# FNet mixing and a low-rank mixer: symmetric DFT tables from fewer sines, odd part of batch 0 folded first, weights' loads placed behind batch 0, last chunk stored by single tiles

## The chip, the cores and the metric

One core of one Trainium2 chip runs the program alone. The metric is device time in microseconds (us) per execution; the time before is the median of three runs. One more execution was taken with the hardware profiler, and all views below are of that one.

## The reference

x is 8 x 3136 x 256 in float32. A two-dimensional Fourier transform over rows and channels gives its real part, then a mixer adds a product of rank 32 along the rows, and a two-layer product along the channels:

```python
X = np.fft.fft(x, axis=1)
X = np.fft.fft(X, axis=2)
x = X.real
xt = x.transpose(0, 2, 1)
h = xt @ U @ V                         # U 3136 x 32, V 32 x 3136
u = x + h.transpose(0, 2, 1)
ch = np.maximum(u @ w_ch1, 0.0) @ w_ch2   # 256 x 1024 and 1024 x 256
out = u + ch
```

## The kernel before

The real part of the transform is (cosine over rows)(cosine over channels) minus (sine)(sine). The kernel makes the tables on the chip, folds the input by symmetry so that each product is short, and transforms with matmuls.

**Input.** For a batch b, `load_x(b)` brings x into `xf` (rows forward, two halves a, gathered by POOL's indirect DMAs, L52) and into `xr` (rows backward, plain loads on SP's queue, L69). `load_0` fills one more partition of both by two small loads on SP (L75, L78). There is one buffer of each, so the next batch's load waits until the fold has read them. U's loads (`uf`, `ur`) run ahead of x's on the same queues.

**Tables.** `tabs[0]` (sine; named tabs in the profile) and `tabs[1]` (cosine; tabc) have 99 partitions, eight row groups i, two frequency parities, and 393 frequencies plus 32 columns. `phase` (VectorE, L139 and L141) makes an angle per element into `ph`; `sine` (ScalarE, L146) is one activation from it, `cosine` two: an absolute value (L152) and a sine (L153). Each of the eight groups is computed in full width, 2 x 393. `halve` (L201) scales the last group. `transform_u` multiplies the tables with the folded U (`fold_u`, L164 to L169) on TensorE (L194) and copies the result into the table's 32 last columns (L196, L197), so that the transform of x also yields the low-rank part.

**Fold.** `fold(b)` on VectorE: `along_d` takes differences (L217) and sums (L218) of mirrored channels from xf into `eof` and from xr into `eor`, and ScalarE copies the two lone channels (L215); `mirror` combines `eof` and reversed `eor` into `eos` (L222, L224); `half` (L228) adds or subtracts the two row halves into `G[b % 2][parity]`. G has the odd (difference) part in columns 0:128, the even (sum) part in 128:256, and the two lone channels in 256:258 with zeros behind them.

**Transforms.** `seq(b, par, typ, pn)` multiplies G with the tables (L279), typ 1 from G's even part (4 matmuls into A), typ 0 from its odd part and the lone channels (4 + 4 matmuls into B). pn = 0 is copied by ScalarE (`ev`, L283), and VectorE combines both pn into A or B (L292 to L297). The order is par 0 typ 1, par 0 typ 0, par 1 typ 1, par 1 typ 0. `chan` does the channel transform (L304 with A, L306 with B, copies L308 into S and T), with its sine and cosine tables `msn` and `mc` made from `pd` in the start and two sign memsets of msn on VectorE (L258, L259). `lowrank` makes TA and one row of VA (L320).

**Chunks.** The output is made in 49 chunks of 512 rows: `front(c)` adds the low-rank part (L342, L350), `first_product` is L362 with the ReLU L364 on ScalarE, `second_product` is L376 into a PSUM pair `p2` of two 128-row tiles; VectorE adds the residual (L382, L384, L385), and one store per chunk goes out on SP (L388).

**Order.** The source writes batch 0 out ahead of everything; then a table `due` spreads each later batch's fold, load and transforms over the chunks of the batch before it. The weights are loaded by POOL's queue behind the first transforms in the source: W1's upper half (L414), W1's lower half gathered in reverse and cast (`w1t`, L52 and L420), W2 (L421), V (L429). The framework sets all semaphores and lays out each engine's queue when the program is built; an instruction need not stand in a queue where the source has it.

Of the kernel before, what the change touches and what calls it, by code (L numbers as in the profile page):

```python
# [16 lines left out]
P = 128  # L17
PQ = 98
# [9 lines left out]
def kernel(  # L28
# [108 lines left out]
    def phase(y, a_ap, col_ap, bits):  # L137

        nc.vector.tensor_scalar(y.bitcast(FP32), a_ap, col_ap, float(2 ** (23 - bits)),  # L139
                                op0=AL.mult, op1=AL.add)  # L140
        nc.vector.tensor_single_scalar(y, y, 2 ** bits - 1, op=AL.bitwise_and)  # L141

    def sine(out_, y, bits, sgn):
        unit = TWO_PI / 2 ** bits
        pp = out_.shape[0]
        nc.scalar.activation(out_, y, AF.Sin, scale=-sgn * unit,  # L146
                             bias=(c_pi if sgn > 0 else c_npi)[:pp])

    def cosine(out_, y, bits):
        pp, free = y.shape  # L150
        ab = gen.tile([pp, free], FP32, tag="ab", name="ab")
        nc.scalar.activation(ab[:], y, AF.Abs, bias=c_half[bits][:pp])  # L152
        nc.scalar.activation(out_, ab[:] if len(out_.shape) == 2 else  # L153
                             ab.rearrange("p (a q) -> p a q", a=2), AF.Sin,
                             scale=TWO_PI / 2 ** bits, bias=c_nhp[:pp])

    kflat = krow.rearrange("p a q -> p (a q)")
    ph = gen.tile([KP, NI, 2 * NQ], I32, name="ph", bufs=1)
    uo = cpool.tile([KP, 2, NI, R], FP32, name="uo")
    ue = cpool.tile([KP, 2, NI, R], FP32, name="ue")  # L160
    GU = [cpool.tile([KP, 2, NI, R], BF16, name=f"gu{par}", tag=f"gu{par}") for par in range(2)]
# [20 lines left out]

    def transform_u(typ):

        for pk in range(2):
            pu = psum.tile([P, NI, R], FP32, tag="dft", name="pu", bufs=3)
            for io in range(NI):
                pn = (io + 1) % 2
                m = kp(io)
                j0 = NQ - 1 - (4 * 97 + (io + 1) // 2)  # L190
                ks = ktiles(pk)
                for n, i in enumerate(ks):
                    w = tabs[typ][:kp(i), i, pn, j0:j0 + 4 * (m - 1) + 1:4]
                    nc.tensor.matmul(pu[:m, io, :], w, GU[pn][:kp(i), typ, i, :],  # L194
                                     start=(n == 0), stop=(n == len(ks) - 1))
# [5 lines left out]
        nc.vector.tensor_single_scalar(tabs[t][:, NI - 1, :, :NQ], tabs[t][:, NI - 1, :, :NQ],  # L201
                                       hv[:KP], op=AL.mult)

    for i in range(NI):
        phase(ph[:, i], kflat[:KP], ncol[:KP, i:i + 1], 15)
        sine(tabs[0][:, i, :, :NQ], ph[:, i].rearrange("p (a q) -> p a q", a=2), 15, 1)
    fold_u()
    halve(0)
    transform_u(0)
    for i in range(NI):  # L210
        cosine(tabs[1][:, i, :, :NQ], ph[:, i], 15)
    def fold(b):

        def along_d(a, src, dst):
            nc.scalar.copy(dst[:, a, :, 128:257:128], src[:, a, :, 0:129:128])  # L215
            lo, hi = src[:, a, :, 1:128], src[:, a, :, 255:128:-1]
            nc.vector.tensor_tensor(dst[:, a, :, 1:128], lo, hi, op=AL.subtract)  # L217
            nc.vector.tensor_tensor(dst[:, a, :, 129:256], lo, hi, op=AL.add)  # L218

        def mirror(a):  # L220
            rv = EOR_[:, a, ::-1]
            nc.vector.tensor_tensor(EOS[:, a, :, 0:128], EOF_[:, a, :, 0:128], rv[:, :, 0:128],  # L222
                                    op=AL.subtract)
            nc.vector.tensor_tensor(EOS[:, a, :, 128:258], EOF_[:, a, :, 128:258],  # L224
                                    rv[:, :, 128:258], op=AL.add)

        def half(par):
            nc.vector.tensor_tensor(G[b % 2][par][:, :, 0:258], EOS[:, 0], EOS[:, 1],  # L228
                                    op=AL.add if par == 0 else AL.subtract)

        for a in range(2):
            yield lambda a=a: along_d(a, xf, EOF_)
            yield lambda a=a: along_d(a, xr, EOR_)
            yield lambda a=a: mirror(a)
        yield lambda: half(0)
        yield lambda: half(1)

    for step in fold(0):
        step()
    halve(1)  # L240
    transform_u(1)


    lrow = cpool.tile([P, 2, P], FP32, name="lrow")
    pcol = cpool.tile([P, 1], FP32, name="pcol")
    nc.gpsimd.iota(lrow[:], pattern=[[0, 2], [1, P]], base=0, channel_multiplier=0,
                   allow_small_or_imprecise_dtypes=True)
    nc.gpsimd.iota(pcol[:], pattern=[[0, 1]], base=0, channel_multiplier=1,
                   allow_small_or_imprecise_dtypes=True)
# [8 lines left out]
    nc.vector.memset(msr[:, :, 0:1], 1.0)  # L258
    nc.vector.memset(msr[:, :, 1:2], -1.0)  # L259
    MDT = [MSN, MC]  # L260

    def seq(b, par, typ, pn):

# [100 lines left out]
        nc.scalar.activation(k["h"][:, j, :], p1[:], AF.Relu)  # L364

    def second_product(c, t):
        k = CK[c]
        h, ut = k["h"], k["ut"]
        if t == 0:
            k["o"] = cp.tile([P, CH // P, D], FP32, tag="o", name="o", bufs=2)  # L370
        if t % 2 == 0:
            k["p2"] = psum.tile([P, 2, D], FP32, tag="p2", name="p2", bufs=2)
        o, p2 = k["o"], k["p2"]
        rs = slice(t * P, (t + 1) * P)
        for j in range(JT):
# [111 lines left out]
```

## Time and profile before

| what | us |
|---|---|
| median of 3 runs (lowest, highest) | 508.53 (507.36, 508.66) |
| the profiled execution | 507.78 |
| its span, first to last instruction | 506.0 |
| PE busy | 475.2 (94%) |
| VectorE (DVE) busy | 309.5 (61%) |
| ScalarE (ACT) busy | 288.7 (57%) |
| POOL busy | 38.7 (8%) |
| first product (L362) starts | 54.58 |
| last output add (L385) ends | 501.68 |

The page divides the span into 40 slices of 12.65 us; each digit is the busy share in tenths:

```profile
PE   0559999999999999999999999999999999999995
DVE  8874999999999776963474345344343344343432
```

In a list by order of time a line gives start, length, engine, line of the kernel, operation and tiles, the count of merged instructions, and in brackets how long the engine idled before it and what released it. In a list of waits the three numbers are the sum, the count and the longest. PEld is TensorE's weight load; a name with q is a queue's own instruction.

### The profile page before, as it was taken

How to read it: one execution, taken by the hardware profiler on the slowest of the kernel's cores; microseconds unless marked ns; L12 is line 12 of the kernel's file. 1: busy time of each engine (PE TensorE's matmuls, PEld its weight loads, DVE VectorE, ACT ScalarE, POOL GpSimd, SP SyncE). 2: the span in 40 equal slices, each digit the busy share in tenths (PEclk: the TensorE clock that was granted, in tenths of full speed). 3: DMA queues.
4: the chain of work that ended last, by engine and by line, in shares of the span. 5: the costliest groups of instructions: out<-in, count | busy, mean ns of one | idle time of the engine just before them, and what ended most of it. 6: DMA issues, size and time to landing. Idle time of an engine off the chain costs nothing.

```text
span 506.0 us, 8152 instructions
## 1 busy us (share of the span) xinstructions
PE 475.2 (94%) x3152; PEld 305.7 (60%) x3152; DVE 309.5 (61%) x681; ACT 288.7 (57%) x565; POOL 38.7 (8%) x45
## 2 busy tenths in 40 slices
PE   0559999999999999999999999999999999999995
PEld 0544466666666666666666666666666666666664
DVE  8874999999999776963474345344343344343432
ACT  6672754766466644755456544755466545665561
POOL 8250111002120100000000000000000000000000
PEclk9999999999999999999999999999999999999998
DMA  7856786789959982334223342333224322333442
GB/s 207 185 135 155 131 239 183 212 233 244 225 168 228 297 212 93 92 99 121 64 62 84 105 83 62 105 85 105 62 63 99 104 71 63 104 87 107 120 115 93
DMA packets 83422, 67.13 MB, mean 133 GB/s; under 512 B 53418, under 2 KB 79856, under 8 KB 80232
## 3 DMA queue, kind: packets, MB, share of 16 engines
q1 hardware_dynamic: 79816, 51.86, 39.0%
q0 software_dynamic: 3568, 14.76, 11.2%
q8 instruction: 24, 0.39, 0.3%
q14 instruction: 14, 0.11, 0.1%
HBM read 29.26 MB, written 25.69 MB: 109 GB/s over the span
## 4 chain that ended last, share of the span: by engine, by line
PE 93%; ACT 3%; DMA 1%; DVE 1%; POOL 0%; issue 0%; DVEq 0%; POOLq 0%; ACTq 0%
PE p L376 34%; PE p L362 34%; PE pt L279 14%; PE ph L342 4%; PE pu L194 2%; PE pst L306 2%; PE pst L304 2%; DMA uf<-in_moe_U_dram,xidx 1%; ACT ab L152 1%; ACT tabc L153 1%; PE ptt L316 1%; DVE tabs L201 0%; ACT S L308 0%; ACT T L308 0%; POOL uf L52 0%
## 5 line engine op out<-in xcount | busy, mean ns | idle before, releaser
L364 ACT ACTIVATE h<-p 128x512 bf16<-128x512 f32 x392 | 218.3, 597 | 141.7 <-PE p L362 141.6
L362 PE MATMUL p<-u,w 128*128 128x512 bf16 x784 | 209.7, 379 | 0.6 <-DVE u L350 0.5
L376 PE MATMUL p<-w,h 128*128 128x256 bf16 x1568 | 203.5, 273 | 0.0
L376 PEld LDWEIGHTS <-h 128*128 128x128 bf16 x1568 | 153.3, 98 | 59.0
L362 PEld LDWEIGHTS <-w 128*128 128x128 bf16 x784 | 75.7, 98 | 63.4 <-issue 3.3
L382 DVE TENSOR_TENSOR o<-p,ut 128x4 f32<-128x4 f32 x98 | 15.9, 162 | 138.5 <-PE p L376 137.0
L279 PE MATMUL pt<-tabc,g 98*128 98x425 bf16 (+1 forms) x256 | 58.0, 352 | 0.4 <-ACT tabc L196 0.4
L279 PEld LDWEIGHTS <-g 98*128 98x128 bf16 (+1 forms) x384 | 38.1, 99 | 31.3 <-issue 3.7
L384 DVE TENSOR_TENSOR o<-p,ut 128x254 f32<-128x254 f32 x98 | 40.2, 411 | 0.0
L385 DVE TENSOR_TENSOR o<-p,ut 128x254 f32<-128x254 f32 x98 | 40.2, 410 | 0.0
L283 ACT COPY ev<-pt 128x425 f32<-128x425 f32 x32 | 16.5, 516 | 36.7 <-PE pt L279 27.4
L350 DVE TENSOR_TENSOR u<-ph,S 128x512 bf16<-128x512 f32 (+15 forms) x64 | 34.9, 555 | 0.9 <-PE ph L342 0.9
L350 DVE TENSOR_TENSOR u<-ph,T 128x512 bf16<-128x512 f32 (+15 forms) x64 | 34.8, 554 | 0.0
L52 POOL DMA_INDIRECT xf<-in_x_dram,xidx x16 | 23.3, 1455 | 123.5 <-ACT h L364 69.9
L342 PE MATMUL ph<-va,ta 128*128 128x512 bf16 (+18 forms) x128 | 29.3, 329 | 0.6 <-ACT ta L319 0.6
L279 PE MATMUL pt<-tabs,g 98*128 98x425 bf16 (+1 forms) x128 | 29.1, 350 | 0.0
L292 DVE TENSOR_TENSOR B<-pt,ev 128x393 bf16<-128x393 f32 (+1 forms) x16 | 9.3, 584 | 24.5 <-PE pt L279 24.2
L306 PE MATMUL pst<-B,msn 128*128 128x392 bf16 (+1 forms) x64 | 20.9, 330 | 0.4 <-DVE B L292 0.4
L304 PE MATMUL pst<-A,mc 128*128 128x392 bf16 (+1 forms) x64 | 21.0, 331 | 0.1
L308 ACT CAST S<-pst 128x392 bf16<-128x392 f32 (+1 forms) x32 | 15.8, 493 | 8.8 <-PE pst L306 8.7
L217 DVE TENSOR_TENSOR eof<-xf 99x1016 bf16<-99x1016 f32 x16 | 19.3, 1206 | 2.3 <-DMA xf<-in_x_dram 2.0
L292 DVE TENSOR_TENSOR A<-pt,ev 128x393 bf16<-128x393 f32 (+1 forms) x16 | 9.4, 589 | 17.8 <-PE pt L279 17.8
(79 smaller groups left out, 278.0 us busy)
## 6 DMA issues: line engine op xcount, KB each, us to landing
out_dram<-o SPq DMA_DIRECT2D x49, 512.0 KB
xr<-in_x_dram SPq DMA_DIRECT2D x16, 784.0 KB
ut<-u SPq DMA_TRANSPOSE x49
w<-in_moe_w_ch_dram POOLq DMA_DIRECT2D x1, 512.0 KB, 13.0
va<-in_moe_V_dram POOLq DMA_DIRECT2D x2, 196.0 KB, 3.2
xf<-in_x_dram,xidx POOLq DMA_INDIRECT x16, 8.8
w<-in_moe_w_ch_dram POOLq DMA_DIRECT2D x1, 256.0 KB, 12.4
ur<-in_moe_U_dram SPq DMA_DIRECT2D x1, 196.0 KB
```

Of the source, the lines that this page charges most:

```text
L52: nc.gpsimd.indirect_dma_start(out_, None, bass.AP(t.tensor, t.offset, [[w, rows], [1, w]]), bass.IndirectOffsetOnAxis(idx, 0), element_of ...
L217: nc.vector.tensor_tensor(dst[:, a, :, 1:128], lo, hi, op=AL.subtract)
L279: nc.tensor.matmul(pt[:], g[:kp(i), i, col:col + P], tabs[t][:kp(i), i, par, :], start=(n == 0), stop=(n == len(mm) - 1))
L304: nc.tensor.matmul(pt[:, :hi - lo], MC[:, h * P:(h + 1) * P], d["A"][:, lo:hi], start=True, stop=False)
L306: nc.tensor.matmul(pt[:, :hi - lo], MSN[:, h * P:(h + 1) * P], d["B"][:, lo:hi], start=False, stop=True)
L342: nc.tensor.matmul(ph[:, col:col + hi - lo], TA[b % 2][:, s * P:(s + 1) * P], VA[b % 2][:, lo:hi], start=True, stop=True)
L350: nc.vector.tensor_tensor(u[:, s, col:col + hi - lo], ph[:, col:col + hi - lo], src, op=AL.add)
L362: nc.tensor.matmul(p1[:], W1[:, s, j * P:(j + 1) * P], k["u"][:, s, :], start=(s == 0), stop=(s == 1))
L364: nc.scalar.activation(k["h"][:, j, :], p1[:], AF.Relu)
L376: nc.tensor.matmul(p2[:, t % 2, :], h[:, j, rs], W2[:, j, :], start=(j == 0), stop=(j == JT - 1))
L384: nc.vector.tensor_tensor(o[:, ts, 1:P], p2[:, :, 1:P], ut[:, ts, 1:P], op=AL.add)
L385: nc.vector.tensor_tensor(o[:, ts, P + 1:D], p2[:, :, P + 1:D], ut[:, tT, P - 1:0:-1], op=AL.add)
```

## The change

The source changes at four places.

1. Tables. Of the eight groups, the four with even i still get a full sine. The other four get a sine over half of the frequencies plus the middle one, and `mirror_even` copies the rest on ScalarE, read backwards, with a sign. For the cosine, the groups with even i are copied from the sine table, read backwards (`cosine_odd`); the others are computed over half and mirrored. A memset clears each table's first column. `halve(0)` stands ahead of `fold_u`, and `transform_u` takes parity 1 first. The angle `pd` of the channel tables is made ahead of `fold_u`, msn and mc right behind the cosines, and msn's two sign memsets go to POOL.
2. Batch 0's fold is written out: first all differences and what follows from them (`half` on columns 0:128 and 256:258), with the lone channels on VectorE, then the sums. `halve(1)` stands inside it, `transform_u(1)` behind it. Batch 0's transforms run typ 0 first for both parities; later batches keep their order, and their `fold` does the same work as before.
3. Two one-column copies on POOL that read xf and xr (`gate`) stand ahead of the weights' loads in the source.
4. The last chunk's second products use one PSUM tile per 128 rows, with a store for each.

```diff
+    gate = cpool.tile([P, 2], FP32, name="gate")
...
+    lrow = cpool.tile([P, 2, P], FP32, name="lrow")
+    pcol = cpool.tile([P, 1], FP32, name="pcol")
+    nc.gpsimd.iota(lrow[:], pattern=[[0, 2], [1, P]], base=0, channel_multiplier=0,
+                   allow_small_or_imprecise_dtypes=True)
+    nc.gpsimd.iota(pcol[:], pattern=[[0, 1]], base=0, channel_multiplier=1,
+                   allow_small_or_imprecise_dtypes=True)
...
-    ph = gen.tile([KP, NI, 2 * NQ], I32, name="ph", bufs=1)
+    NH = NQ // 2 + 1
+    pho = gen.tile([KP, NI // 2, 2, NQ], I32, name="pho", bufs=1)
+    phe = gen.tile([KP, NI // 2, 2, NH], I32, name="phe", bufs=1)
...
-        for pk in range(2):
+        for pk in (1, 0):
...
-    for i in range(NI):
-        phase(ph[:, i], kflat[:KP], ncol[:KP, i:i + 1], 15)
-        sine(tabs[0][:, i, :, :NQ], ph[:, i].rearrange("p (a q) -> p a q", a=2), 15, 1)
-    fold_u()
-    halve(0)
-    transform_u(0)
-    for i in range(NI):
-        cosine(tabs[1][:, i, :, :NQ], ph[:, i], 15)
...
-    for step in fold(0):
-        step()
-    halve(1)
-    transform_u(1)
+    def cells(t, i, col, step, n, skew):
+
+        v = tabs[t][:, i, :, :]
+        return bass.AP(v.tensor, v.offset + col, [v.ap[0], [QW + skew, 2], [step, n]])
+
+    def mirror_even(t, i):
+
+        odd_m = (i + 1) // 2 % 2 == 1
+        sgn = 1.0 if odd_m == (t == 0) else -1.0
+        nc.scalar.activation(cells(t, i, 0, 1, NH - 1, 1), cells(t, i, NQ - 1, -1, NH - 1, 0),
+                             AF.Copy, scale=sgn)
+
+    def cosine_odd(i):
+
+        nc.scalar.activation(cells(1, i, 1, 1, NQ - 1, 0), cells(0, i, NQ - 2, -1, NQ - 1, 1),
+                             AF.Copy, scale=1.0 if i % 4 == 0 else -1.0)
+
+    for t in tabs:
+        nc.vector.memset(t[:, :, :, 0:1], 0.0)
+    for m, i in enumerate(range(0, NI, 2)):
+        phase(pho[:, m], krow[:KP], ncol[:KP, i:i + 1], 15)
+        sine(tabs[0][:, i, :, :NQ], pho[:, m], 15, 1)
+    for m, i in enumerate((7, 5, 3, 1)):
+        phase(phe[:, m], krow[:KP, :, NH - 1:], ncol[:KP, i:i + 1], 15)
+        sine(tabs[0][:, i, :, NH - 1:NQ], phe[:, m], 15, 1)
+        mirror_even(0, i)
...
+    phase(pd[:], lrow.rearrange("p a l -> p (a l)"), pcol[:], 17)
+
+    halve(0)
+    fold_u()
+    transform_u(0)
+    for i in range(0, NI, 2):
+        cosine_odd(i)
+    for m, i in enumerate((7, 5, 3, 1)):
+        cosine(tabs[1][:, i, :, NH - 1:NQ], phe[:, m], 15)
+        mirror_even(1, i)
     sine(MSN[:, 0:128], pd[:, 0:128], 17, -1)
     sine(MSN[:, 128:256], pd[:, 128:256], 17, 1)
     cosine(MC[:], pd[:], 17)
...
-    nc.vector.memset(msr[:, :, 0:1], 1.0)
-    nc.vector.memset(msr[:, :, 1:2], -1.0)
+    nc.gpsimd.memset(msr[:, :, 0:1], 1.0)
+    nc.gpsimd.memset(msr[:, :, 1:2], -1.0)
...
+    for a in range(2):
+        for src, dst in ((xf, EOF_), (xr, EOR_)):
+            along_d(a, src, dst, 0)
+            nc.vector.tensor_copy(dst[:, a, :, 128:257:128], src[:, a, :, 0:129:128])
+        mirror(a, slice(0, 128), AL.subtract)
+        mirror(a, slice(256, 258), AL.add)
+        if a == 0:
+            halve(1)
+    for par in range(2):
+        half(0, par, slice(0, 128))
+        half(0, par, slice(256, 258))
+    for a in range(2):
+        for src, dst in ((xf, EOF_), (xr, EOR_)):
+            along_d(a, src, dst, 1)
+        mirror(a, slice(128, 256), AL.add)
+    for par in range(2):
+        half(0, par, slice(128, 256))
+    transform_u(1)
...
+        w = 1 if c == NCH - 1 else 2
...
-        if t % 2 == 0:
+        if t % w == 0:
             k["p2"] = psum.tile([P, 2, D], FP32, tag="p2", name="p2", bufs=2)
...
-        if t == CH // P - 1:
+        if w == 1:
+            nc.sync.dma_start(out=out_f[c * CH + t * P:c * CH + (t + 1) * P, :], in_=o[:, t, :])
+        elif t == CH // P - 1:
             nc.sync.dma_start(
                 out=out_f[c * CH:(c + 1) * CH, :].rearrange("(t p) d -> p t d", p=P), in_=o[:])
...
-        for par in range(2):
-            for typ in (1, 0):
-                for pn in range(2):
-                    yield lambda par=par, typ=typ, pn=pn: seq(b, par, typ, pn)
+        for par, typ in ([(0, 0), (1, 0), (0, 1), (1, 1)] if b == 0 else
+                         [(0, 1), (0, 0), (1, 1), (1, 0)]):
+            for pn in range(2):
+                yield lambda par=par, typ=typ, pn=pn: seq(b, par, typ, pn)
...
+    for t, s_ in ((xf, 0), (xr, 1)):
+        nc.gpsimd.tensor_copy(gate[:PQ, s_:s_ + 1], t[:PQ, 1, 0, 0:1])
     nc.gpsimd.dma_start(out=W1[:, 0, :], in_=moe_w_ch1[0:P, :])
```

More of the change, by code (lines that the diff above doesn't have):

```diff
@@ L149, in cosine @@
     def cosine(out_, y, bits):
-        pp, free = y.shape
-        ab = gen.tile([pp, free], FP32, tag="ab", name="ab")
+        pp = y.shape[0]
+        ab = gen.tile(list(y.shape), FP32, tag="ab", name="ab")
         nc.scalar.activation(ab[:], y, AF.Abs, bias=c_half[bits][:pp])
[L153 to L157, printed above, removed]
-    ph = gen.tile([KP, NI, 2 * NQ], I32, name="ph", bufs=1)
+        nc.scalar.activation(out_, ab[:], AF.Sin, scale=TWO_PI / 2 ** bits, bias=c_nhp[:pp])
+    NH = NQ // 2 + 1
+    pho = gen.tile([KP, NI // 2, 2, NQ], I32, name="pho", bufs=1)
+    phe = gen.tile([KP, NI // 2, 2, NH], I32, name="phe", bufs=1)
     uo = cpool.tile([KP, 2, NI, R], FP32, name="uo")
@@ L202, in halve @@
                                        hv[:KP], op=AL.mult)
-    for i in range(NI):
-        phase(ph[:, i], kflat[:KP], ncol[:KP, i:i + 1], 15)
-        sine(tabs[0][:, i, :, :NQ], ph[:, i].rearrange("p (a q) -> p a q", a=2), 15, 1)
-    fold_u()
-    halve(0)
-    transform_u(0)
-    for i in range(NI):
-        cosine(tabs[1][:, i, :, :NQ], ph[:, i], 15)
[L212 to L236, printed above, removed]
@@ L238 @@
-    for step in fold(0):
-        step()
-    halve(1)
-    transform_u(1)
[L244 to L249, printed above, removed]
+    def cells(t, i, col, step, n, skew):
+        v = tabs[t][:, i, :, :]
+        return bass.AP(v.tensor, v.offset + col, [v.ap[0], [QW + skew, 2], [step, n]])
@@ L257, with along_d, alone, mirror @@
     msr = MSN[0:1].rearrange("p (l two) -> p l two", two=2)
-    nc.vector.memset(msr[:, :, 0:1], 1.0)
-    nc.vector.memset(msr[:, :, 1:2], -1.0)
+    nc.gpsimd.memset(msr[:, :, 0:1], 1.0)
+    nc.gpsimd.memset(msr[:, :, 1:2], -1.0)
     MDT = [MSN, MC]
+    def along_d(a, src, dst, part):
+        lo, hi = src[:, a, :, 1:128], src[:, a, :, 255:128:-1]
+        if part == 0:
+            nc.vector.tensor_tensor(dst[:, a, :, 1:128], lo, hi, op=AL.subtract)
+        else:
+            nc.vector.tensor_tensor(dst[:, a, :, 129:256], lo, hi, op=AL.add)
+    def alone(a, src, dst):
+        nc.scalar.copy(dst[:, a, :, 128:257:128], src[:, a, :, 0:129:128])
+    def mirror(a, cols, op):
+        nc.vector.tensor_tensor(EOS[:, a, :, cols], EOF_[:, a, :, cols],
+                                EOR_[:, a, ::-1][:, :, cols], op=op)
+    def half(b, par, cols):
+        nc.vector.tensor_tensor(G[b % 2][par][:, :, cols], EOS[:, 0, :, cols],
+                                EOS[:, 1, :, cols], op=AL.add if par == 0 else AL.subtract)
+    def fold(b):
+        def both(a, src, dst):
+            alone(a, src, dst)
+            for part in range(2):
+                along_d(a, src, dst, part)
+        for a in range(2):
+            yield lambda a=a: both(a, xf, EOF_)
+            yield lambda a=a: both(a, xr, EOR_)
+            yield lambda a=a: (mirror(a, slice(0, 128), AL.subtract),
+                               mirror(a, slice(128, 258), AL.add))
+        for par in range(2):
+            yield lambda par=par: half(b, par, slice(0, 258))
+    for a in range(2):
[9 more added lines that the diff above has]
+        half(0, par, slice(256, 258))
+    for a in range(2):
+        for src, dst in ((xf, EOF_), (xr, EOR_)):
+            along_d(a, src, dst, 1)
+        mirror(a, slice(128, 256), AL.add)
+    for par in range(2):
+        half(0, par, slice(128, 256))
+    transform_u(1)
     def seq(b, par, typ, pn):
@@ L375, in second_product @@
         for j in range(JT):
-            nc.tensor.matmul(p2[:, t % 2, :], h[:, j, rs], W2[:, j, :],
+            nc.tensor.matmul(p2[:, t % w, :], h[:, j, rs], W2[:, j, :],
                              start=(j == 0), stop=(j == JT - 1))
-        if t % 2 == 0:
+        if t % w != w - 1:
             return
-        ts = slice(t - 1, t + 1)
-        tT = slice(CH // P + t - 1, CH // P + t + 1)
-        nc.vector.tensor_tensor(o[:, ts, 0:P + 1:P], p2[:, :, 0:P + 1:P],
+        ts = slice(t + 1 - w, t + 1)
+        tT = slice(CH // P + t + 1 - w, CH // P + t + 1)
+        nc.vector.tensor_tensor(o[:, ts, 0:P + 1:P], p2[:, :w, 0:P + 1:P],
                                 ut.rearrange("p (s t) c -> p t s c", s=2)[:, ts, :, 0], op=AL.add)
-        nc.vector.tensor_tensor(o[:, ts, 1:P], p2[:, :, 1:P], ut[:, ts, 1:P], op=AL.add)
-        nc.vector.tensor_tensor(o[:, ts, P + 1:D], p2[:, :, P + 1:D], ut[:, tT, P - 1:0:-1],
+        nc.vector.tensor_tensor(o[:, ts, 1:P], p2[:, :w, 1:P], ut[:, ts, 1:P], op=AL.add)
+        nc.vector.tensor_tensor(o[:, ts, P + 1:D], p2[:, :w, P + 1:D], ut[:, tT, P - 1:0:-1],
                                 op=AL.add)
-        if t == CH // P - 1:
+        if w == 1:
+            nc.sync.dma_start(out=out_f[c * CH + t * P:c * CH + (t + 1) * P, :], in_=o[:, t, :])
+        elif t == CH // P - 1:
             nc.sync.dma_start(
                 out=out_f[c * CH:(c + 1) * CH, :].rearrange("(t p) d -> p t d", p=P), in_=o[:])
+        if t == CH // P - 1:
             del CK[c]
```

## The prediction

> **What bounds the kernel now.** I read the page's shares first, then the chain of waits, then busy time by stage, then each engine's order of time up to the first product and over the last chunk. By stage (columns: length; busy time and instructions of PE, PEld, DVE, ACT, POOL; clock; DMA share; GB/s):
>
> ```profile
> 36.90:42.40 5.50, 5.44 (x17) 2.32 (x17) 1.84 (x5) 1.60 (x5) 0.00 (x0) 1.00 1.01 223
> 42.40:48.30 5.90, 5.90 (x34) 3.15 (x33) 2.28 (x6) 1.55 (x3) 0.00 (x0) 1.00 0.65 164
> 54.50:69.10 14.60, 14.42 (x86) 8.37 (x86) 14.60 (x21) 9.50 (x21) 2.41 (x2) 1.00 0.91 201
> 69.10:500.00 430.90, 430.90 (x2863) 276.92 (x2861) 255.01 (x586) 247.25 (x490) 13.98 (x10) 1.00 0.47 127
> ```
>
> From 54.5 to 500 PE has no hole to fill, and the change takes no matmul away. Only the 54.6 us before the first product and the 5 us behind the last matmul can shrink. The chain of waits through the start (start, length, what):
>
> ```profile
> 14.53 1.93 DVE tabs L201
> 16.50 4.62 PE pu L194 x48
> ...
> 28.40 1.68 ACT ab L152 x2
> 30.98 5.54 PE pu L194 x58
> 36.96 11.48 PE pt L279 x48
> ```
>
> ScalarE's cosine table ends at 30.9, PE needs 5.5 us for `transform_u(1)`, and the batch-0 matmuls (L279) wait for that. VectorE's fold of batch 0 is a second road to the same place: it starts at 18.44, when the row load of xf has landed, and was held three times:
>
> ```profile
> DVE eof L217 <- DMA xf<-in_x_dram: 2.0, 1, 2.0
> DVE msn L258 <- ACT msn L146: 1.6, 1, 1.6
> DVE tabc L201 <- ACT tabc L153: 1.0, 1, 1.0
> ```
>
> Once the cosines are no longer last, VectorE's road decides. In order of time:
>
> ```profile
> 21.09 1.22 DVE L217 TENSOR_TENSOR eof<-xf 99x1016 bf16<-99x1016 f32 x1 [0.31 <-DMA xf<-in_x_dram,xidx]
> 22.22 1.21 DVE L218 TENSOR_TENSOR eof<-xf 99x1016 bf16<-99x1016 f32 x1
> ...
> 24.14 1.21 DVE L217 TENSOR_TENSOR eor<-xr 99x1016 bf16<-99x1016 f32 x1
> ...
> 49.59 1.20 DVE L217 TENSOR_TENSOR eof<-xf 99x1016 bf16<-99x1016 f32 x1
> 50.71 1.21 DVE L218 TENSOR_TENSOR eof<-xf 99x1016 bf16<-99x1016 f32 x1
> 52.84 0.96 DVE L320 TENSOR_TENSOR va<-S,T 1x1567 bf16<-1x1567 bf16 x1 [0.93 <-ACT T L308]
> ```
>
> The queues do not keep the source's order: both halves of xf were folded before xr, and batch 1's fold (49.59) stands ahead of batch 0's `va`. An instruction that was expected to wait was passed by later ones when the program was laid out.
>
> **The change part by part.** *Tables on ScalarE.* Starts of 786-wide activations are 0.84 apart; a 256-wide one took 0.51 and a 786-wide one 0.95, so I estimate 0.52 for 394 wide. Sines: 8 x 0.84 = 6.7 before, 4 x 0.84 + 4 x (0.52 + 0.52 for the mirror copy) = 7.5 after. Cosines: 16 x 0.84 = 13.4 before, 4 x 0.84 + 4 x 3 x 0.52 = 9.6 after. The sines still end at about 12, the cosines at 12 + 9.6 + 0.9 for the pu copies = 22.5 instead of 30.9. A copy that reads backwards on ScalarE is not in the trace. Bounds: 0.35 (the 98x224 copy) and 0.95 (a 786-wide sine) for a 392-wide mirror, up to twice 0.84 for an odd row. At the upper end ScalarE ends near 29; I take 0.52, since VectorE's reversed reads (L217) cost what their forward neighbours cost.
>
> *Tables on VectorE.* Phases go from 8 x 1.02 to 4 x 1.02 + 4 x 0.63 (by the 256-wide pair, 0.35 and 0.29), plus pd's 0.7 and two column memsets of 0.1. `halve(0)` moves ahead of `fold_u`. All of it lies before U's landing (`fold_u` starts at 11.89), which hides it. The pcol iota now stands before U's gathers on POOL: +0.1. `transform_u(0)` then runs from 14.3 to 20.4 instead of to 21.1; `transform_u(1)`, 3.1 us for each half, can take its odd half at once and its even half from 23.5 to 26.6, with its copy done at 27.0.
>
> *Fold of batch 0.* Steps: a difference 1.13 (start to start), the lone columns now on VectorE 0.1 (not in the trace for this form; bounds 0.07 from a 128x1 memset and 0.27 from ScalarE's cast), a 128-column mirror or half 0.60, a two-column piece 0.1, `halve(1)` 0.4. I assume the order stays as before where sources arrive: xf first, both parts. So 21.09 (xf's second half lands, 7.42 + 13.6) + 1.23 + 0.4 + 2 x 1.13 for xf's even parts + 1.23 for xr + (0.60 + 0.85 + 0.1) + 1.23 + 0.7 + 0.7 for the first parity's half = 30.4. The 0.85 is POOL's cast of W1: in before a mirror beside it took 1.52 instead of 0.68. PE starts at 30.5 instead of 36.96: -6.5. The even rest (2 x 1.13 + 2 x 0.6 + 2 x 0.6, the second odd half 0.7 and one B eviction 1.06) ends at 36.9, while PE is busy with the 32 odd matmuls until 38.8 (5.4 us for 16 slow ones, then 0.18 each): hidden, with 1.9 to spare. Without that cover it would cost its 4.7.
>
> The Trainium skill, "SBUF — State Buffer", section Who interferes with whom, says that a VectorE instruction with two SBUF inputs and a GpSimd one that reads SBUF exclude each other for a whole instruction. The 1.52 against 0.68 agrees; without the rule the sum would be 0.85 lower.
>
> The first window above has 17 matmuls in 5.5 us and the second 34 in 5.9, both at a granted clock of 1.00. I leave the same slow stretch in the sum of after, since PE also idles ahead of it there. The Trainium skill, "TensorE: Matmul & The Clock Gate", Part 1, gives about 3.4 us of half clock after an idle stretch. By that the stretch would be 2 us shorter and I should gain 1 us more; this trace shows 5.4 us, so I do not count it.
>
> *From the transforms on.* A comes last now instead of B, so the two cosine matmuls that stood ahead of the wait come behind it: +0.17. The first channel matmul with both inputs moves from 49.16 to 42.85: -6.3, and the first product from 54.58 to 48.3. The sign memsets of msn go to POOL, which waits there for W1's rows until 25.6 anyway.
>
> *What is late next.* Batch 1. Its gathers were issued at 32.22 and 34.05 and landed 15.2 and 16.6 us later (47.4 and 50.6). POOL is free at 30.5, so they may come 1 to 1.7 us earlier. From its first difference (49.59) to G's first half, VectorE needed 18.9 us: 12.6 of fold, `va` 0.96, six u adds 3.6, output adds 0.7, 0.9 idle. If `va` and two u adds go first (46.5 to 48.7), the fold and the rest (12.6 + 2.4 + 0.7) end at 64.4; PE wants it at 69.13 - 6.3 = 62.8. So 0 to 1.6 us are given back: the start gains 4.7 to 6.3, and I take 5.5.
>
> *Weights' loads.* The gate copies wait for xf and xr, but nothing ties the W1 load (L414) to them except POOL's order, and that order let W2's load pass a memset that stands earlier in the source:
>
> ```profile
> 11.27 0.98 POOL L421 DMA_DIRECT2D w<-in_moe_w_ch_dram  x1
> 12.23 0.09 POOL L417 MEMSET pint<- 1x1 int32 x1
> ```
>
> So I expect the loads where they were and cost the gate at nothing: POOL waits from 16.2 to 25.6 for W1's gathered rows in any case. Without that cover, queued behind the gates (21.1) are that gather, its cast, V's loads and batch 1's gathers.
>
> *Tail.* The last store goes out after the last add (501.68) and moves 524 KB; the fine DMA view shows 0.35 MB per us, 1.5 us. A 128-row tile is a quarter: -1.1. The last two adds are half as wide (0.41 each; a start distance of 0.33 becomes about 0.2): -0.3. One p2 buffer per tile: PE may wait 0.1 for an eviction. Sum -1.3, bounds -0.9 and -1.6.
>
> **Sum.** 5.5 + 1.3 = 6.8 off the profiled 507.78 is 501.0. That execution lies 0.75 under the median of 508.53, so the forecast is **501.7**, its own range 500.5 to 503.
>
> **Rivals.**
> A, *batch 1 in the way*: its first difference still stands ahead of `va`, as in before. Then `va` waits for the load. The load has its row parts on SP too, and those are no freer than before, so I move 49.59 by no more than 2.4 to 47.2; the idle 0.9 goes: start -3.3, in all -4.6, **503.9**. For it: the trace's own order. Against: in after `va` is ready 6 us sooner, the load hardly.
> B, *order as written, loads held*: x lands near 17.5 and the odd part is ready at 25; then ScalarE and `transform_u(1)` bound PE at 27.0. Batch 1 gives some back: start -8, **499.2**. Against: the POOL rows above.
> C, *slower*: batch 1's first difference stands ahead of A's evictions, in VectorE's idle time between transforms. They then wait for the load: 47.4 + 2.25 + 1.6 = 51.3 for A's first half against 49.1, +2.2 - 1.3, **509.4**, and 510.9 if the load comes 1.5 later. It turns into a loss once the load lands after 46.5. Against: in before the idle gaps at 41 and 47 were not filled that way.
> D, *start unchanged*: backward copies at their upper end, or another order, eat the start's gain; only the tail stays, **507.2**.
>
> **Chances.** Forecast 0.45, A 0.22, B 0.16, C 0.08, D 0.09. About 0.3% (1.5 us) can be told from no change. Faster by more: the first three and a third of D, 0.86; within: 0.06; slower: 0.08. The range 497.5 to 506.5 holds the first three with their spreads and leaves out D and C, 0.17.
>
> **What would show it.** Cosines done near 22.5 on ScalarE; xf's even parts ahead of xr; first L279-type matmul near 30.5 with sine operands; first product near 48.3; PE's wait before batch 1's transforms under 2 us; W1's load still near 9; last stores of 128 KB. It is wrong if batch 1's fold comes before `va`, if POOL holds the weights back, or if backward copies take twice my 0.52.

## The result, and the profile after

| | before | after |
|---|---|---|
| median, us (lowest, highest; runs) | 507.36 (507.22, 508.66; 6) | 510.98 (510.05, 512.24; 6) |
| the profiled execution, its span | 507.78, 506.0 | 510.05, 508.3 |
| first transform matmul (L279; now L329) | 36.96 | 31.83 |
| first product (L362; now L412) | 54.58 | 58.59 |
| last matmul's end to the span's end | 5.2 | 3.3 |

The ratio is 1.0066 [1.0045, 1.0086]: slower by some 3.4 us (3.6 by the medians, that of before now being of six runs), where 6.8 less was forecast. The transforms do start 5.1 us earlier, but the first product, which needs their result, starts 4.0 us later than before. All of the loss lies between these two rows. From the first product to the end of the span the kernel is 1.7 us shorter (449.7 against 451.4), nearly all of it in the tail.

Busy time by stage of the changed kernel (columns as in the prediction: length; PE, PEld, DVE, ACT, POOL; clock; DMA share; GB/s):

```profile
38.80:43.70 4.90, 3.90 (x21) 1.92 (x20) 1.73 (x4) 0.63 (x2) 0.00 (x0) 1.00 0.90 219
43.70:47.30 3.60, 0.02 (x1) 0.00 (x0) 1.80 (x4) 0.62 (x2) 0.96 (x1) 0.74 0.47 132
47.30:51.00 3.70, 3.00 (x8) 1.16 (x8) 1.67 (x5) 0.53 (x2) 0.00 (x0) 0.50 0.64 199
51.00:55.60 4.60, 4.50 (x14) 2.02 (x14) 3.98 (x6) 2.83 (x6) 0.93 (x1) 0.50 0.01 2
58.50:69.00 10.50, 10.36 (x58) 5.71 (x59) 10.50 (x17) 7.54 (x17) 0.00 (x0) 1.00 0.82 181
```

PE stands still for 3.6 us in the middle of batch 0's transforms, and for the 8.3 us that follow (47.36 to 55.64) its granted clock is 0.50. Who held it is in the list of waits of 30 to 60 us (sum, count, longest):

```profile
ACT eof L267 <- DMA xf<-in_x_dram,xidx: 10.6, 2, 6.7
...
PE pt L329 <- ACT ev L333: 4.7, 2, 3.6
...
DVE eof L261 <- DMA xf<-in_x_dram,xidx: 3.2, 1, 3.2
```

The order of time of ScalarE, VectorE and PE shows the same from the side of the queues:

```profile
42.15 0.26 ACT L267 CAST eof<-xf 99x16 bf16<-99x16 f32 x1 [6.75 <-DMA xf<-in_x_dram,xidx]
42.28 0.51 ACT L333 COPY ev<-pt 128x425 f32<-128x425 f32 x1
46.68 0.26 ACT L267 CAST eof<-xf 99x16 bf16<-99x16 f32 x1 [3.90 <-DMA xf<-in_x_dram,xidx]
46.80 0.51 ACT L333 COPY ev<-pt 128x425 f32<-128x425 f32 x1
```
```profile
42.11 1.22 DVE L261 TENSOR_TENSOR eof<-xf 99x1016 bf16<-99x1016 f32 x1 [3.17 <-DMA xf<-in_x_dram,xidx]
43.24 1.21 DVE L263 TENSOR_TENSOR eof<-xf 99x1016 bf16<-99x1016 f32 x1
44.37 0.57 DVE L342 TENSOR_TENSOR B<-pt,ev 128x392 bf16<-128x392 f32 x1
```
```profile
42.84 0.88 PE L329 MATMUL pt<-tabc,g 98*128 98x425 bf16 x4 [1.00 <-ACT ev L333]
47.36 3.00 PE L329 MATMUL pt<-tabc,g 98*128 98x425 bf16 x8 [3.65 <-ACT ev L333]
```

A copy of two lone channels of batch 1 (L267, 0.26 us of work) stands in ScalarE's queue ahead of a copy of batch 0 to `ev`, and waits 6.75 us for batch 1's rows; a second one waits 3.90. Until `ev` is copied, the PSUM tile is not free, so PE's next four or eight matmuls wait as well. VectorE has the same fault: batch 1's first difference stands ahead of batch 0's second B eviction. The chain of waits of after runs through it:

```profile
33.73 12.87 DMA xf<-in_x_dram,xidx
...
46.68 0.06 ACT eof L267
...
46.80 0.52 ACT ev L333
...
47.36 3.01 PE pt L329 x8
```

In before this stretch of the chain was one unbroken piece of 48 matmuls, 11.48 us long.

### The profile page after: what moved, and what is told of

It reads as the page before. It is cut to its first block, busy times and chain, and to the rows that moved or that the text cites. A ratio compares the mean times of both kernels' runs of the same rounds, so it can differ in the third digit from the quotient of the medians.

```text
span 508.3 us, 8117 instructions
## 1 busy us (share of the span) xinstructions
PE 476.6 (94%) x3097; PEld 306.7 (60%) x3152; DVE 308.3 (61%) x697; ACT 283.9 (56%) x565; POOL 39.7 (8%) x49
## 4 chain that ended last, share of the span: by engine, by line
PE 89%; DMA 5%; DVE 3%; issue 1%; POOL 1%; ACT 0%; DVEq 0%; POOLq 0%; ACTq 0%
PE p L428 34%; PE p L412 33%; PE pt L329 13%; DMA xf<-in_x_dram,xidx 5%; PE ph L392 4%; PE pst L354 2%; PE pst L356 2%; PE ptt L366 1%; POOL uf L52 0%; DVE eor L261 0%; DVE eof L263 0%; DVE eor L263 0%; DVE eos L270 0%; DVE eor L296 0%; POOL xf L52 0%
## 5 line engine op out<-in xcount | busy, mean ns | idle before, releaser
L412 PE MATMUL p<-u,w 128*128 128x512 bf16 x735 | 202.1, 379 | 2.3 <-DVE u L400 0.6
L412 PEld LDWEIGHTS <-w 128*128 128x128 bf16 x784 | 75.8, 98 | 63.5 <-issue 3.5
L434 DVE TENSOR_TENSOR o<-p,ut 128x4 f32<-128x4 f32 (+1 forms) x100 | 16.3, 163 | 138.0 <-PE p L428 137.1
L329 PE MATMUL pt<-tabc,g 98*128 98x425 bf16 (+1 forms) x256 | 59.3, 357 | 4.7 <-ACT ev L333 4.7
L329 PEld LDWEIGHTS <-g 98*128 98x128 bf16 (+1 forms) x384 | 38.6, 101 | 37.4 <-issue 10.1
L436 DVE TENSOR_TENSOR o<-p,ut 128x254 f32<-128x254 f32 (+1 forms) x100 | 40.5, 405 | 0.0
L437 DVE TENSOR_TENSOR o<-p,ut 128x254 f32<-128x254 f32 (+1 forms) x100 | 40.5, 405 | 0.0
L329 PE MATMUL pt<-tabs,g 98*128 98x425 bf16 (+1 forms) x128 | 30.4, 362 | 0.6 <-DVE g L274 0.6
L392 PE MATMUL ph<-va,ta 128*128 128x512 bf16 (+14 forms) x122 | 28.2, 327 | 0.8 <-ACT ta L369 0.5
L261 DVE TENSOR_TENSOR eof<-xf 99x1016 bf16<-99x1016 f32 x16 | 19.3, 1209 | 7.1 <-DMA xf<-in_x_dram,xidx 7.1
L354 PE MATMUL pst<-A,mc 128*128 128x392 bf16 (+1 forms) x64 | 22.6, 353 | 0.7 <-DVE A L342 0.7
L356 PE MATMUL pst<-B,msn 128*128 128x392 bf16 (+1 forms) x64 | 22.5, 352 | 0.0
L270 DVE TENSOR_TENSOR eos<-eof,eor 99x1024 bf16<-99x1024 bf16 (+2 forms) x34 | 21.0, 656 | 0.1
```

The lines of the kernel that those rows point to most:

```text
L270: nc.vector.tensor_tensor(EOS[:, a, :, cols], EOF_[:, a, :, cols], EOR_[:, a, ::-1][:, :, cols], op=op)
L329: nc.tensor.matmul(pt[:], g[:kp(i), i, col:col + P], tabs[t][:kp(i), i, par, :], start=(n == 0), stop=(n == len(mm) - 1))
L354: nc.tensor.matmul(pt[:, :hi - lo], MC[:, h * P:(h + 1) * P], d["A"][:, lo:hi], start=True, stop=False)
L356: nc.tensor.matmul(pt[:, :hi - lo], MSN[:, h * P:(h + 1) * P], d["B"][:, lo:hi], start=False, stop=True)
L392: nc.tensor.matmul(ph[:, col:col + hi - lo], TA[b % 2][:, s * P:(s + 1) * P], VA[b % 2][:, lo:hi], start=True, stop=True)
L412: nc.tensor.matmul(p1[:], W1[:, s, j * P:(j + 1) * P], k["u"][:, s, :], start=(s == 0), stop=(s == 1))
```

## The experiments

"Held" below means that steps of batch 1's fold may not be laid out ahead of a named instruction of batch 0; apart from e4's two gate copies, no kernel leaves work out. They ran in four groups (e1 to e4; e5 to e9; e10 to e13; e15), each beside the kernel before on the same chip: 507.55, 507.63, 507.79 and 508.17 us. The first product's start is from each kernel's trace.

| kernel | median us | ratio to before | first product |
|---|---|---|---|
| e1 tail alone, on before | 506.40 | 0.9972 [0.9961, 0.9984] | 55.13 |
| e2 batch 1's fold held | 503.14 | 0.9908 [0.9886, 0.9930] | 49.97 |
| e3 only ScalarE's lone copies held | 514.79 | 1.0149 [1.0129, 1.0170] | 57.07 |
| e10 only VectorE's part held | 510.54 | 1.0050 [1.0033, 1.0066] | 57.32 |
| e4 no gate copies | 511.42 | 1.0083 [1.0063, 1.0104] | 59.56 |
| e5 loads of batch 1 early | 502.82 | 0.9902 [0.9885, 0.9918] | 51.01 |
| e7 early loads, and held | 502.42 | 0.9892 [0.9874, 0.9911] | 51.31 |
| e8 as e2, old order of batch 0's fold | 506.35 | 0.9970 [0.9958, 0.9981] | 53.77 |
| e9 as e2, old tables | 508.15 | 1.0005 [0.9994, 1.0016] | 54.26 |
| e12 gates, then loads of batch 1, then weights | 504.87 | 0.9947 [0.9917, 0.9976] | 53.66 |
| e13 as e12, and held | 501.67 | 0.9882 [0.9865, 0.9898] | 50.16 |
| e15 as e13, late even part of xr | 500.68 | 0.9855 [0.9840, 0.9871] | 49.16 |

**e1.** The kernel before with the change's last part alone.

```diff
+        w = 1 if c == NCH - 1 else 2
...
+        if w == 1:
+            nc.sync.dma_start(out=out_f[c * CH + t * P:c * CH + (t + 1) * P, :], in_=o[:, t, :])
```

> The kernel before with only the last chunk's single-tile products and stores. Theory: the end of the span behind the last matmul shrinks from 5.4 to about 3.6 us, less 0.2 us that PE waits for a PSUM tile, so about 505.8 (505.2 to 506.3). Rival (the tail hides nothing, the last landing is set by something else): 507.4, no change.

506.40: 1.2 us less than before by the medians, 1.4 by the ratio, and just above the range that was expected. The tail is worth what the sum said, and is no part of the loss.

**e2, e3, e10: which queue blocks.** e2 holds all eight fold steps of batch 1 on both engines, e3 with `act` alone, e10 with `dve` alone:

```diff
+        last_act = nc.scalar.copy(TA[b % 2][:R, :], pt[:])
+        last_dve = nc.vector.tensor_tensor(VA[b % 2][R:R + 1, HALF + 1:S], d["S"][0:1, HALF - 1:0:-1],
...
+        if b == 0:
+            HOLD.update(act=last_act.ins, dve=last_dve.ins)
...
+    def held(step):
+        with ExitStack() as stack:
+            for k in ('act', 'dve'):
+                stack.enter_context(tc.issue_after(HOLD[k]))
+            step()
...
+        if b == 1:
+            steps[:8] = [lambda s=s: held(s) for s in steps[:8]]
```

> The changed kernel, with batch 1's fold held behind batch 0's last eviction (TA's copy on ScalarE, VA's row on VectorE) in the two queues. Theory Q (the order of the queues lost the time): PE's waits of 1.2 and 3.8 us on ev and the half-speed stretch behind them (some 4 us) go, first product near 49.6 to 50.5 instead of 58.6; VectorE gives 1 to 2 us back in batch 1's fold; 502 to 504. Rival L (batch 1's load is what is late, wherever the wait stands): the wait moves to batch 1's transforms, 508.5 to 511.

> The changed kernel, with only ScalarE's copies of batch 1's lone channels held back; VectorE's queue stays as in the changed kernel. If the copies ahead of ev are the cause: ev is on time, VectorE's difference still waits until 42.1 and B's second eviction ends near 45.4, PE waits up to 2 us for a PSUM buffer: 504 to 506. If VectorE's difference is the cause: 509 to 511.

> The changed kernel with only VectorE's part of batch 1's fold held behind batch 0's VA row; ScalarE's lone copies (L267) stay where the changed kernel has them, ahead of two of batch 0's copies to ev. Theory Q (either queue alone blocks batch 0): the copies to ev come again at about 42.3 and 46.8 us behind the landing of batch 1's rows, PE waits 1 and 3.6 us for them, the channel matmuls run at half clock, first product 57 to 58.5, time 508.5 to 511. Rival V (the differences on VectorE did the harm, the lone copies only came along): first product near 50, time 503 to 504.

With both held, PE in order of time never waits for batch 1 until the second products of the first chunk:

```profile
39.77 3.87 PE L329 MATMUL pt<-tabc,g 98*128 98x425 bf16 x20
44.37 0.33 PE L354 MATMUL pst<-A,mc 128*128 128x393 bf16 x1 [0.74 <-DVE A L342]
...
49.97 1.46 PE L414 MATMUL p<-u,w 128*128 128x512 bf16 x6 [0.60 <-DVE u L402]
62.72 1.92 PE L430 MATMUL p<-w,h 128*128 128x256 bf16 x16 [1.17 <-DVE o L439]
66.30 0.38 PE L414 MATMUL p<-u,w 128*128 128x512 bf16 x1 [0.31 <-ACT h L416]
```

Between the first transform matmul and the first product lie 18.06 us here and 26.76 in after. The 8.7 us are: 4.65 of waits for `ev`; 1.4 for the last eight transform matmuls (3.00 against 1.61 for eight elsewhere in the same trace); 1.9 for the channel matmuls and the low-rank step (6.1 against 4.2), both at half clock; and 0.5 for a slow first stretch that lasted longer (the first 36 matmuls took 10.0 us against 9.5); some 0.2 is left over. Held, the kernel gives 1.17 + 0.31 back at 62.7 and 66.3: the output add that PE waits for there (L439, 62.25) stands in VectorE's queue behind four late fold steps of batch 1 (57.34 to 61.85).

e3 missed its expectation. With ScalarE clear, VectorE alone blocks:

```profile
43.88 1.22 DVE L261 TENSOR_TENSOR eof<-xf 99x1016 bf16<-99x1016 f32 x1 [5.21 <-DMA xf<-in_x_dram,xidx]
45.01 1.21 DVE L263 TENSOR_TENSOR eof<-xf 99x1016 bf16<-99x1016 f32 x1
46.14 0.57 DVE L342 TENSOR_TENSOR B<-pt,ev 128x392 bf16<-128x392 f32 x1
```

The B eviction comes at 46.14, and PE waits 4.76 us in one piece for it. The same happens once more a batch later, when batch 2's differences (72.25 to 75.62) stand ahead of an A eviction of batch 1:

```profile
75.62 0.58 DVE L342 TENSOR_TENSOR A<-pt,ev 128x393 bf16<-128x393 f32 x1
...
76.81 0.90 PE L329 MATMUL pt<-tabs,g 98*128 98x425 bf16 x4 [1.69 <-DVE tab L347]
```

PE waits 1.69 us there, and from 78.20 to 81.20 its granted clock is 0.50 again. So 514.79 is more than the start explains. e10, with VectorE clear, has the waits of after on ScalarE:

```profile
41.06 0.26 ACT L267 CAST eof<-xf 99x16 bf16<-99x16 f32 x1 [5.70 <-DMA xf<-in_x_dram,xidx]
...
46.58 0.26 ACT L267 CAST eof<-xf 99x16 bf16<-99x16 f32 x1 [4.89 <-DMA xf<-in_x_dram,xidx]
46.70 0.92 ACT L333 COPY ev<-pt 128x425 f32<-128x425 f32 x2
```

So either queue alone is enough to lose, and only clearing both frees PE: the losses do not add, they cover each other.

**e4: the gate.** The two copies that wait for xf and xr are left out.

```diff
-    for t, s_ in ((xf, 0), (xr, 1)):
-        nc.gpsimd.tensor_copy(gate[:PQ, s_:s_ + 1], t[:PQ, 1, 0, 0:1])
```

> The changed kernel without the two gate copies on POOL. Theory Q: batch 1's gathers are issued within 1 us of where they are, so the waits stay and the time stays at 510 to 511.5. Rival L (the gate delays POOL and with it batch 1's gathers): 506 to 508.

511.42, as after within the intervals. The fold of batch 0 now ends 2 us later (first transform matmul at 33.82 instead of 31.83): without the gate, POOL's memsets of g and va run at 13.67 to 15.58, and one step of `pd` on VectorE beside them takes 2.59 us to the next start instead of 0.20, ahead of all that follows.

```profile
13.30 2.67 DVE L148 TENSOR_SCALAR pd<-pd 128x256 int32<-128x256 int32 x1
15.89 0.41 DVE L207 TENSOR_SCALAR tabs<-tabs,hv 99x786 bf16<-99x786 bf16 x1
```

Yet the time is nearly the same, since batch 1's gathers (32.12 and 33.69) go out when they did and set the end. The gate is not the cause of the loss; it is worth 2 us at the start, and in after these are waited away.

**e5, e7, e12, e13: rows that are there in time.** e5 moves batch 1's loads behind batch 0's fold; e7 adds a hold, behind batch 0's last `ev` copy and last eviction only; e12 places the gate copies ahead of these loads, and e13 is e12 with e7's hold. The cut is e12's; e5 has only the two `load_x` lines of it, at the same places.

```diff
+    for t, s_ in ((xf, 0), (xr, 1)):
+        nc.gpsimd.tensor_copy(gate[:PQ, s_:s_ + 1], t[:PQ, 1, 0, 0:1])
+    load_x(1)
     transform_u(1)
...
-    load_x(1)
     front(0)
```

> The changed kernel with batch 1's load written right behind batch 0's fold, ahead of the weights in the source; nothing is held in the queues. The gathers should be issued near 25 instead of 32.4 and 33.7 and land before 40. Theory Q with it: batch 1's lone copies still stand ahead of ev, but what they wait for is there, so PE's waits on ev shrink under 1 us in all: 502 to 505. Rival (the place in the queue costs, whatever the load does): 508 or more.

> As the run with the early load, and batch 1's fold held behind batch 0's last ev copy and last eviction only, so that VectorE can use its idle time during the channel transform (3.4 us in the run held behind VA's row). Theory: first product near 50 as there, and the 1.2 us that PE lost later to VectorE's batch 1 work goes: 501 to 502.5. Rival (that wait has another cause): 503 or more.

> The changed kernel with batch 1's loads issued right behind the two gate copies and ahead of all loads of the weights; nothing is held. Theory Q (what counts is only whether batch 1's rows have landed when its queued steps come up): the gathers go out near 23 to 25 us instead of 32.4 and 33.7, land before 42, no copy to ev waits for them, first product 50 to 51, no wait of PE behind it for batch 1, time 501 to 503. Rival W (the weights, now last, become late): W1's second half, gathered behind batch 1's rows, lands after 50 us, the first product waits for it, time 503 to 506.

> As the kernel before it in this batch, and batch 1's fold also held behind batch 0's last copy to ev and last eviction. Theory Q: with the rows landed early the hold has nothing left to save, so within 0.7 us of that kernel, 501 to 503. Rival: if VectorE's batch 1 work between batch 0's evictions still costs PE time, the hold gains 1 us or more.

With the gathers out at 23.11 and 25.08 instead of 32.40 and 33.73, e5 loses nothing to its queues, with the same fold steps in it. Hold and early rows are two cures of one fault: from the first transform matmul to the first product, e2 takes 18.06 us, e5 17.72 and e7, with both, 17.66, against 26.76 in after. The totals of e5 and e7 alone would not show it, because both kernels start the transforms late (33.29 and 33.65): as in e4, a step of `pd` runs beside a memset of POOL (2.42 and 2.10 us long). e12 missed: its gathers went out at 25.96 and 27.23, but one lone copy was laid out still further ahead, and the rows came at 41.86 in the profiled execution:

```profile
41.86 0.26 ACT L267 CAST eof<-xf 99x16 bf16<-99x16 f32 x1 [6.39 <-DMA xf<-in_x_dram,xidx]
41.98 0.51 ACT L336 COPY ev<-pt 128x425 f32<-128x425 f32 x1
```

PE waited 2.55 us there, and soon after its clock fell to half (0.50 from 43.40 to 46.30). That the weights come later in e12 is not the reason: W1 is cast by 30.0. Ten runs of e12 lie from 502.50 to 508.78; that its time hangs on when the rows land is a reading of this, since only one of them has a trace. e13 takes the wait and the spread away, 501.67 (501.45 to 502.44), so the expectation that the hold adds nothing there was wrong too, by the same cause. e13 starts its first product when e2 does (50.16 and 49.97) and has no wait behind it; that is the 1.5 us between them.

**e8, e9: what the two start edits are worth once the queues are clear.** e8 is e2 with batch 0 folded and transformed in the old order; e9 is e2 with the eight full-width sines and cosines of before.

```diff
+    for step in fold(0):
+        step()
+    halve(1)
...
+        for par, typ in [(0, 1), (0, 0), (1, 1), (1, 0)]:
```
```diff
+    for i in range(NI):
+        phase(ph[:, i], krow[:KP], ncol[:KP, i:i + 1], 15)
+        sine(tabs[0][:, i, :, :NQ], ph[:, i], 15, 1)
...
+    for i in range(NI):
+        cosine(tabs[1][:, i, :, :NQ], ph[:, i], 15)
```

> The changed kernel with the queues held as in e2_hold, but batch 0 folded in the order of before (differences and sums together, ScalarE's lone copies, typ 1 first). If folding the odd part first is worth what the prediction gave it, PE's first transform moves from 31.9 to about 35 (the even rest of 4 us is no longer behind it): 505 to 507. If VectorE's whole fold bounds in either order: 503 to 504.

> The changed kernel with the queues held as in e2_hold, but the tables made in full width with two activations per cosine as in before. If the tables mattered, ScalarE's cosines end near 31 again, transform_u(1) near 36.5, and PE starts the transforms there: 506 to 508. If they are hidden behind the fold: 503 to 504.

By the ratios, against e2, the new fold is worth 3.2 us (e8 takes all of the second place back: order, lone columns, `halve(1)` and the order of the transforms) and the tables 5.0. But neither gives anything alone: with one of them missing, 506.35 and 508.15 are no better than the tail by itself (e1, 506.40). Some 1.5 us of that is the hold's, since both wait at its late output add as e2 does. The rest is two roads that end close together: in before the first half of G was done at 36.3 and `transform_u(1)` at 36.5, in after at 31.83 and 31.2. With the old fold, e8's transforms start at 35.71, and with the old tables, e9's `transform_u(1)` runs till 37.4 though G's first half was ready at 30.45. Each road hides what the other gains.

**e15: the term of the fold.** As e13, with the even sums of xr and their mirrors held behind the odd halves of G.

```diff
-        for src, dst in ((xf, EOF_), (xr, EOR_)):
-            along_d(a, src, dst, 1)
-        mirror(a, slice(128, 256), AL.add)
+        along_d(a, xf, EOF_, 1)
+        with tc.issue_after(odd.ins):
+            along_d(a, xr, EOR_, 1)
+            mirror(a, slice(128, 256), AL.add)
```

> As the version with early loads and a hold (501.67 us), and in batch 0's fold the even sums of xr and their mirrors are held behind the odd halves of G, as the forecast's sum had them. Theory T (the fold was 1.73 us longer than forecast because one even sum, 1.13, and one even mirror, 0.60, were placed ahead of G's odd half; behind the fold the second half of transform_u(1) is next in line, its last matmul ending near 31.2): G's first odd half starts near 29.4 instead of 31.1, but the first transform matmul only at 31.2 to 31.4 instead of 31.8, so 0.4 to 0.6 us faster, 501.0 to 501.3. Rival (VectorE alone sets that start): first matmul near 30.1, 500.0. If the even part no longer fits behind the odd matmuls, the B evictions come late and the time is 502 or more.

```profile
28.63 3.14 PE L200 MATMUL pu<-gu,tabc 98*98 98x32 bf16 x32 [0.87 <-ACT tabc L219]
31.61 2.29 PE L333 MATMUL pt<-tabs,g 98*128 98x425 bf16 x6
```

The first transform matmul follows `transform_u(1)` with no idle time: VectorE is no longer last there, though xf's rows landed 0.6 us later in this execution than in e13's. The gain is larger than that theory's 0.4 to 0.6: 500.68 against 501.67 (taken on different chips; by the ratios 0.9855 and 0.9882, 1.4 us, with intervals that touch). The start moved by 0.21 only; the transforms took 11.78 us to the first channel matmul instead of 12.57, with a shorter slow stretch (4.2 us at a pitch of 0.354 instead of 6.0). Whether that shortening is caused by the order or by chance is open. This is the fastest version: 1.45% [1.29, 1.60] under the kernel before.

## Why the prediction was wrong

**The step that failed** is the choice under *What is late next*: "If `va` and two u adds go first". It put batch 1's fold behind all of batch 0, and set rival C, batch 1's first difference ahead of batch 0's evictions, at 0.08 because "in before the idle gaps at 41 and 47 were not filled that way". In after they are: L261 stands ahead of a B eviction, and ScalarE's lone copies ahead of two `ev` copies. They waited for batch 1's rows (6.75 and 3.90 us), PE waited 4.65 us for `ev`, and its clock fell to half. The text itself had read from before that the queues do not keep the source's order, and that an instruction expected to wait is passed by later ones; it then took the old order as evidence for a program in which the gaps lie elsewhere. e2 restores the order that the forecast assumed and gives 503.14, outside "its own range 500.5 to 503": 4.4 us below its before by the medians, 4.7 by the ratio, where 6.8 were forecast. So the failed step is most of the miss, but not all. The other 2 us are in e2's trace: the first product starts at 49.97 instead of 48.3, as the transforms start 1.4 late, and 1.48 is given back instead of 0.8.

**What C missed.** Its price, 509.4 or 510.9 with a late load, is near the 510.98, but for other reasons; that is luck. It knew only VectorE, and turned "into a loss once the load lands after 46.5"; the first half of the rows, which VectorE waited for, was there at 42.1. ScalarE's lone copies (L267) were in no sum; the second of them waited for the second half, till 46.6, and e10 shows that they alone cost as much. And it had no half clock: taking 1.4 and, against e2, 1.9 out of after's span leaves 505.0, 1.0 less than before's and so less than the 1.7 gained behind the first product. The waits alone would thus have used up the start's gain; the clock made the whole a loss. That is arithmetic on the traces; no run kept the clock up through a wait this long, and e12's fell after a shorter one.

**Start of the transforms**, forecast 30.5, measured 31.83. VectorE in order of time:

```profile
20.30 1.22 DVE L261 TENSOR_TENSOR eof<-xf 99x1016 bf16<-99x1016 f32 x1 [1.61 <-DMA xf<-in_x_dram,xidx]
21.44 0.20 DVE L296 CAST eof<-xf 99x16 bf16<-99x16 f32 x1
21.52 2.33 DVE L263 TENSOR_TENSOR eof<-xf 99x1016 bf16<-99x1016 f32 x2
23.78 1.21 DVE L261 TENSOR_TENSOR eor<-xr 99x1016 bf16<-99x1016 f32 x1
24.90 0.93 DVE L296 CAST eor<-xr 99x16 bf16<-99x16 f32 x1
24.99 1.04 DVE L207 TENSOR_SCALAR tabc<-tabc,hv 99x786 bf16<-99x786 bf16 x1
25.95 0.75 DVE L270 TENSOR_TENSOR eos<-eof,eor 99x1024 bf16<-99x1024 bf16 x2
26.63 1.20 DVE L261 TENSOR_TENSOR eor<-xr 99x1016 bf16<-99x1016 f32 x1
27.75 1.04 DVE L296 CAST eor<-xr 99x16 bf16<-99x16 f32 x1
28.68 1.20 DVE L263 TENSOR_TENSOR eor<-xr 99x1016 bf16<-99x1016 f32 x1
29.81 1.36 DVE L270 TENSOR_TENSOR eos<-eof,eor 99x1024 bf16<-99x1024 bf16 x3
31.09 1.36 DVE L274 TENSOR_TENSOR g<-eos 99x1024 bf16<-99x1024 bf16 x3
```

By starts, against the forecast's terms: xf's rows 0.8 earlier; `halve(1)` 0.96 instead of 0.4, beside POOL's memset of va (+0.6); POOL's cast of W1 fell on a lone copy (0.93 to the next start instead of 0.1, +0.8) and not on the mirror (-0.9); and one even sum of xr (1.13) and one even mirror (0.60) stand ahead of G's first half, where the sum had them behind (+1.7). Together +1.4, against +1.3 measured. xf's even parts before xr held as forecast. e15 removes the 1.7 and the first matmul then follows `transform_u(1)` at once. The slow first stretch, carried over at 5.4 us, lasted 6.7 in after. That it ran "at a granted clock of 1.00" was no reading: the trace has no clock record before the stretch ends.

**Tables on ScalarE.** The price was about right, the end was not. The cosines' activations take 8.8 us by their starts against a forecast of 9.6 (a backward 392-wide copy 0.42 start to start and a 784-wide one 0.75, not 0.52 and 0.84 or more), but ended at 28.0 instead of 22.5. The reason given for 0.52 did not hold what it said: L217 and L218 of before both read one input backwards, so neither is the other's forward neighbour. The copies themselves settle it. ScalarE idled in between, as its copies of `transform_u(0)`'s results stand ahead of the cosines:

```profile
17.93 0.35 ACT L202 CAST tabs<-pu 98x224 bf16<-98x224 f32 x1 [4.73 <-PE pu L200]
...
20.82 0.36 ACT L202 CAST tabs<-pu 98x224 bf16<-98x224 f32 x1 [1.33 <-PE pu L200]
```

The same waits were in before (4.46 and 0.38); the sum left them out. The result: `transform_u(1)` ended at 31.2, within 0.6 us of becoming the bound, which no term had foreseen.

**Weights' loads.** Forecast near 9 and the gate at nothing; POOL's order in after:

```profile
20.34 1.22 POOL L471 COPY gate<-xf 98x1 f32<-98x1 f32 x1 [6.09 <-DMA xf<-in_x_dram,xidx]
...
22.26 1.39 POOL L52 DMA_INDIRECT w1t<-in_moe_w_ch_dram,pint  x1 [0.17 <-issue]
```

W1's first half went out at 12.59 behind the gate for xr, and its gather at 22.26 behind the gate for xf (13.0 before). The forecast of the order was wrong. That it costs nothing was right, and it even gains 2 us at the start, by keeping POOL's memsets away from VectorE's `pd` (e4). The gain that the text gave POOL, gathers "1 to 1.7 us earlier", did not come: 32.40 and 33.73 against 32.22 and 34.05.

**Given back, tail.** Forecast: 0 to 1.6 us at 62.8, of which the sum took 0.8. In after PE has no such wait, since batch 1's fold ran ahead; e2, with the order that the forecast assumed, gives back 1.48 at 62.7 and 66.3. The tail: -1.3 forecast, -1.2 to -1.4 in e1, and in after's trace 1.9 less behind the last matmul with 0.2 more for the last 40 matmuls.

## What to carry to other kernels

Ask of every engine's queue, not only the busiest one's, which instruction that waits for a load stands ahead of the one that frees PE's PSUM tile: a 0.26 us copy cost 7 us (e10 against e2). The order that a framework lays out belongs to one program and is no evidence for a changed one; where it matters, write it down in the source as a dependence, or have the data there in time, and best both (e13 against e12). When a stage is shortened, move the next stage's loads with it, or the time saved becomes a wait.

## What the runs showed of the hardware

In these traces a PE that waited 1.69 us or more fell to half clock, and stayed there long. After waits of 3.65 us (after), 3.44 (e10), 4.76 (e3) and 4.82 (e4) the channel matmuls started 0.327 us apart instead of 0.166. Shorter waits were enough too: after 2.55 us (e12) the clock was 0.50 from 43.40 to 46.30, after 1.69 (e3, second wait) from 78.20 to 81.20. After 1.00 (after), 1.17 (e2) and 1.18 (e8) it did not fall. In after the 0.50 lasted 8.3 us from PE's restart at 47.36, although PE was busy for 7.5 of them. The Trainium skill, "TensorE: Matmul & The Clock Gate", Part 1, puts the fall at one idle window of about 3.4 us and the way back at about 3.4 us of sustained work. Here 1.69 and 2.55 us of waiting were enough for the fall, and in after the way back took longer; what decides between them is open.

The first transform matmuls of every trace start 0.354 us apart for 4.2 to 6.7 us before they reach 0.18, the same pitch as the later ones at half clock. The traces hold no clock record for that stretch, and the 1.00 printed there is no reading. So the column alone does not show a slow stretch; the pitch does.

Some of VectorE's work took much longer beside work of POOL, casts and memsets alike. A copy of 99 x 16 elements on VectorE takes 0.08 us to the next start, and 0.93 when POOL casts W1 beside it; in e2 the same cast fell on a difference (L261, 2.00 instead of 1.13). The 128 x 256 step of `pd` takes 0.20, and 2.59 beside POOL's memsets (e4); `halve(1)` takes 0.34 with hardly any POOL work beside it (e5), and 0.96 (after) or 1.43 (e4) beside a memset.
